# Attention's transposes as pairs of 64 rows, one slot for both products with v, and five edits behind them

## The chip, the core and the metric

The kernel runs on one core of a Trainium2 chip. Its engines work side by side: TensorE (PE in the rows; its weight loads are PEld), VectorE (DVE), ScalarE (ACT), GpSimd (POOL), and SyncE (SP), which issues most of the DMAs. Each engine takes its instructions in program order and waits on semaphores for what the others produce. The metric is the time of one execution on the device in microseconds (us); lower is better.

## The reference

Attention over 32 heads, a first layer, and a second layer in which each token goes to one of 8 experts:

```python
scores = np.matmul(q, k.transpose(0, 1, 3, 2)) / np.sqrt(64)   # q, k, v: 4 x 8 x 576 x 64
decay = cum[..., :, None] - cum[..., None, :]    # cum: running sum of log f
attn = softmax(where(causal, -1e9, scores + decay))
x = (attn @ v).transpose(0, 2, 1, 3).reshape(2304, 512)
h = x @ w_in                                     # 512 x 2048
x = np.maximum(0.01 * h, h) @ w_out              # 2048 x 512
# tokens take experts greedily, in the order of all logits x @ w_gate (2304 x 8);
# an expert takes at most 288 tokens
out[mask] = np.maximum(x[mask] @ w1[e], 0) @ w2[e]   # for each expert e; 512 -> 1024 -> 512
```

## The kernel before

**Precision.** Most operands are kept as a high and a low part in a shortened float32, and a product is three matmuls (high·high, low·high, high·low). Who needs an operand therefore makes two copies of it: `high` rounds (ACT or DVE), `low` subtracts the high part from the source (DVE or POOL).

**Attention (0 to 201.7 us)** treats 16 pairs of heads. For each pair TensorE transposes q and k (128 tokens by the 64 columns of both heads, tile `x`, into PSUM tile `s`); ACT makes the high and DVE the low parts (`qh`, `kh`, `ql`, `kl`); the scores are computed twice, once with the queries in the rows to get the row maximum and the sum of exponentials (DVE's `kept<-s,mask`, ACT's `kept`), and once transposed to give `P = exp(...)`. The log of the sums, computed by a series on POOL (tile `ln`, 10 columns), is transposed by one matmul and goes back as a row of the scores' operand (function `rows`). The products with v (`s<-P,vt`) are left in `xt` by `finish` for the two halves of the queries. All of these share four PSUM slots called `s`.

TensorE can work on parts of its array. The scores use 64 rows by 128 columns (form "S": two heads side by side, shown as 64\*128 and counted as x2), the products with v 128 rows by 64 columns (form "V"), and everything else, the transposes too, the whole array (form "A").

**Order.** Attention and the first layer are laid out by a planner, class `Plan`: every operation is given an engine, a duration in ns, a rank and the slots that it takes, a simulation with list scheduling decides the order, and the program keeps that order on each engine (class `InOrder`, whose line L72 is therefore the line of nearly all instructions in the rows). The planner charges `TURN` (200 ns) for a change of TensorE's form, and prefers an operation of the present form when its rank is at most `near` behind. The ranks come from 12 per pair plus constants (`ZP`, `ZO`, `ZA`, `ZH`, ...). In the changed kernel L72 is L73.

**First layer (201.7 to 690.3 us).** Its weights are read, split into parts that sum exactly (`wsq`, `wbits`, `wst` on POOL and DVE), transposed (`T<-ident,wst`), and multiplied by the gate's parts (`T<-wt,wgs`), so that the logits come out of the same numbers as the reference's. At 442.7 us the logits, laid out as `L`, are brought into the token list `W0`. Then the greedy routing runs on DVE, POOL and ACT (generator `routing`, which yields the ns that it wants covered), while TensorE is dealt the second product of the first layer (`acc<-wh,gh`, `acc<-wh,gl`) between the routing's steps. At its end the lists of tokens (`ids`) come out of products `q_misc<-r_ge`, and POOL gathers the tokens `xe` by indirect DMA. Behind them the experts' weights are already split: `wst` (SP's DMA, four buffers), `wh` high (ACT, L359), `wh` low (POOL, L360).

**Experts (690.3 to 915.5 us).** `first` computes the hidden layer of 128 units, `after` the products with w2, `leave` transposes an expert's 288 rows in three groups of 96 and scatters them to `out`. They are ordered by the tile framework's scheduler.

Of the kernel before, what the change touches and what calls it, by code (L numbers as in the profile page):

```python
# [27 lines left out]
ACB = 4  # L28
# [10 lines left out]
ZP, ZO, ZA, ZH, ZL, ZW, DW = -39, -27, 5, -9.5, -10.5, 63, 14.5  # L39
ZS = 5, 5.5, 7, 0.5, 2.5, 11, 11.5  # L40
ZQ = 1
ZT = 0, 7
ZR = 5.5
MW = 1.5, 0.6
LN = -8.262958294867817e-08, 87.99986188054224, 1.833333338331171, -2.9997760462926015, 1.4995521528324076, -0.33310946991454005
FIN = ("act", "vec"), ("vec", "gp")
# [5 lines left out]
ZN = 0.5, 0, -4, 0, 0, 0, -0.5, 0, 0, 0, 0, 0, 0, 0, 2, 0.5  # L52
ZM = -2.5, -0.5, 0, -1, 0, 0, 0, 0, 0, 0, 0, 1, -1.5, 0.5, 4, -4
ZB = 0, -4, -5, 0, 0, 0.5, -0.5, 0, 0, -3, 0, -4, 0.5, 0, 0, -1
# [37 lines left out]
class Plan:  # L92
# [5 lines left out]
    MOVE = 650, 2600  # L98
# [6 lines left out]
    def op(self, eng, ns, fn, needs=(), rank=0.0, takes=(), uses=(), move=0, plain=False, form="A"):  # L105
        o = Op(eng, ns, fn, [x for x in needs if x is not None], rank)
        o.move, o.form = move, form
# [12 lines left out]
        self.ops.append(o)  # L120
        return o
# [4 lines left out]
    def order(self):  # L126
# [100 lines left out]
def tile_kernel(ctx, tc, q, k, v, f, w_in, w_out, w_gate, w1, w2, out):  # L227
# [34 lines left out]

    def weight_ops(op, pieces, z, st, low_on, keep=None, hold=()):
# [7 lines left out]
        def chunk(c, src):  # L271
# [33 lines left out]
            s = op("gp", 800, square, [o], z, ["wsq"], [wb])  # L305
            sq = s.got[0]
            o = op("vec", 202, b0, [o], z, ["wbits"], [wb])
            bb = o.got[0]
            o = op("vec", 335, b1, [o], z, (), [bb, wb])
            o = op("vec", 335, b2, [o], z, (), [bb, wb])  # L310
            s = op("gp", 816, big, [s], z, (), [sq])
            takes = [] if "b" in st else ["wst"]
            o = op("gp", 687, mul, [s, o] + st.get("o", []), z, takes, [sq, bb] + ([st["b"]] if "b" in st else []))
# [199 lines left out]
    with ExitStack() as c1:  # L513
# [64 lines left out]
        VT = [stp.tile([128, 5, 2, D], FT, name=f"vt{i}") for i in range(2)]  # L578
        pads = []
        for n in range(NS):  # L580
# [16 lines left out]
            if n < 2:  # L597
                op("gp", 150, lambda n=n: gp.memset(VT[n][64:, 4], 0.0), (), 12 * n - 90)
# [3 lines left out]
        def prepare(n, own, z):  # L602
# [9 lines left out]
            def load(j, i):  # L612
# [4 lines left out]
                at_q[j].dma_start(x3[j][:, :, i], src[b, h + i, :512].rearrange("(t p) d -> p t d", p=128))  # L617
# [15 lines left out]
            def part(end, z):  # L633
                mine = {}

                def flip():
                    mine[0] = p = bank()
                    if end:
                        pe.transpose(p[:, 0, :128], x3["end"].rearrange("p s d -> p (s d)"), ident)
                        return  # L640
                    for j in range(2):
                        for t in range(4):
                            pe.transpose(p[:, j, 128 * t:128 * t + 128], x3[j][:, t].rearrange("p s d -> p (s d)"), ident)

                def high(j, c0, w, a):
                    hi = (qh[:, 64:] if j else kh)[:, c0:c0 + w]
                    x = mine[0][:, 0, a:a + w] if end else mine[0][:, j]
# [5 lines left out]
                def low(j, c0, w, a):  # L653
                    hi, lo = ((y[:, 64:] if j else y)[:, c0:c0 + w] for y in ((qh, ql) if j else (kh, kl)))
                    x = mine[0][:, 0, a:a + w] if end else mine[0][:, j]
                    vec.scalar_tensor_tensor(lo, x, 0.125 if j else 1.0, hi, op0=OP.mult, op1=OP.subtract)
                if end:
                    o = op("pe", 109, flip, loads["end"], z, ["s"], buf["end"] + list(sets.values()))
# [4 lines left out]
                for j, c0, w, a in ([(0, 512, 64, 0), (1, 512, 64, 64)] if end else [(0, 0, 512, 0), (1, 0, 512, 0)]):  # L663
                    a_ = op("act", 51 + .833 * w, lambda x=(j, c0, w, a): high(*x), [o], z + ZH, (), [tb, sets[j]])
                    outs[j] += [a_, op("vec", 69 + 1.042 * w, lambda x=(j, c0, w, a): low(*x), [a_], z + ZL, (), [tb, sets[j]])]
# [10 lines left out]
        def rows(x, dst, need, z, uses, duse):  # L676
# [3 lines left out]
            def flip():  # L680
                mine[0] = bank()[:10, 0, :128]
                pe.transpose(mine[0], x(), ident)

            def high():
                mine[1] = at.tile([10, 2, 128], FR, name="xr", tag="xr", bufs=2)
                act.copy(mine[1][:, 0], mine[0])

            def low():
                vec.tensor_tensor(mine[1][:, 1], mine[0], mine[1][:, 0], op=OP.subtract)
            o = op("pe", 107, flip, need, z + 1, ["s"], uses)  # L690
# [6 lines left out]
        def offsets(n, own, z):  # L697
# [70 lines left out]
            def ratio():  # L768
                own["ln"] = x = at.tile([128, 4, 10], FT, name="ln", tag="ln", bufs=2)
                act.activation(x[:, 0], own["sm"].bitcast(I32), AF.Copy, scale=LN[0], bias=LN[1])  # L770
                act.activation(x[:, 1], x[:, 0], AF.Exp)

            def ready():
                x = own["ln"]
                gp.tensor_scalar(x[:, 3], own["sm"], 1e-9, None, op0=OP.add)

            def series():
                x, t = own["ln"][:, 2], own["ln"][:, 1]
                gp.tensor_tensor(t, own["ln"][:, 3], t, op=OP.mult)
# [5 lines left out]
                gp.tensor_tensor(x, x, own["ln"][:, 0], op=OP.add)  # L785
# [3 lines left out]
            p = op("gp", 250, ready, tots + [o], z + ZR, (), [sb, lb])  # L789
            o = op("gp", 2200, series, [o, p], z + ZR, (), [nb, sb, lb])  # L790
            own["max"] = rows(lambda: own["ln"][:, 2], lambda l: qr[32 + l:97 + l:64], [o], z + ZR, [lb], kq)

        def attend(n, own, z):
# [18 lines left out]
            def score(name, blocks, z):  # L812
# [24 lines left out]
                for n, (i, f0, f1) in enumerate(blocks):  # L837
                    sel = []
                    if f0 == 128 * i:
                        w = min(128, f1 - f0)  # L840
                        sel = [op("gp", 137 + 1.75 * w, lambda a=col[n], w=w: causal(a, w), acts, z + 4, (), [pb])]
# [5 lines left out]
            def values(half, i, z):  # L847
                need, pb, name, a, e, x, y = W[half, i]

                def product():  # L850
                    if i == 0:
                        own["av", half] = bank()[:, 0]
                    for u in range(2):
                        pe.matmul(own["av", half][64 * u:64 * u + 64, x:y], own["v"][:, i, u], own["P", name][:, u, a:e],
                                  start=i == 0, stop=i == (2, 4)[half])
                o = op("pe", 4 * (e - a) / 2.4 + 12, product, need + vl + R.get(("av", half), []), z, ["s"] if i == 0 else [],
                       [vb, pb] + R.get(("avb", half), []), form="V")
                if i == 0:
                    R["avb", half] = [o.got[0]]
                R["av", half] = [o]  # L860

            def finish(half, z):
# [22 lines left out]
                if rest == "gp":  # L885
                    o = op("gp", 96 + 3.55 * w, lambda: low(1), [o], z + 1, (), [xb])
                    o = op("gp", 148 + 2.1 * w, lambda: low(0), [o], z + 1, (), [xb])
# [38 lines left out]
    with ExitStack() as c1:  # L926
        gtp = c1.enter_context(tc.tile_pool(name="gt1", bufs=1, reuse_waits="tile"))
        raw[:] = gtp, W64[1]
        psp = c1.enter_context(tc.tile_pool(name="ps1b", bufs=1, reuse_waits="tile", space=PSUM))
# [77 lines left out]
    with ExitStack() as c2:  # L1007
# [14 lines left out]
        with tc.tile_pool(name="ps2", bufs=1, reuse_waits="tile", space=PSUM) as psp, \  # L1022
# [21 lines left out]
            lp = psa.tile([128, 512], FT, name="acc", tag="acc", bufs=ACB)  # L1044

            def tokens(g):
                for i in (2 * g, 2 * g + 1):
                    pe.matmul(lp[:, E * i:E * i + E], L[:, 128 * i:128 * i + 128], sel, start=True, stop=True)
            o = [op("pe", 430, lambda g=g: tokens(g), lasts[g:g + 1], 200) for g in range(NG)]
# [373 lines left out]
```

## Time and profile before

| | us |
|---|---|
| median of 3 runs (lowest, highest) | 925.02 (924.19, 928.3) |
| the profiled execution, its own time | 927.42 |
| its span from the first to the last instruction | 925.7 |
| TensorE busy | 889.4 (96%) |
| VectorE, ScalarE, GpSimd busy | 584.0, 416.6, 457.6 |
| first layer's first product, 201.7 to 442.7: TensorE busy | 237.0 of 241.0 |
| experts, 690.3 to 915.5: TensorE busy | 222.5 of 225.2 |

The profiled execution took 2.4 us more than the median, and 1.7 us of it lie outside the span. Busy shares are averages over stages with different limits. TensorE's granted clock was 0.989 of full speed over the span: full nearly everywhere, and half in a few short stretches.

### The profile page before, as it was taken

Reading aid. Unit: us, or ns where it says so; the run is one execution under the profiler, and the core shown is the slowest. Engines: PE = TensorE matmul, PEld = TensorE weight load, DVE = VectorE, ACT = ScalarE, POOL = GpSimd, SP = SyncE. Lnnn points to the kernel's source line nnn. Section 1 sums busy time; section 2 is a strip of 40 time slices with the busy share of each in tenths; the row PEclk is TensorE's granted clock in tenths of the full one; section 3 lists DMA queues with packets and bytes.
Section 4 is the critical chain, followed back from the end, with each engine's and each line's share of the span. In section 5 each row is a group of like instructions: output and inputs, shape, how many; then the busy total and the mean of one; then the engine's idle time right before and its main releaser. Section 6 shows DMA issues by size and latency. Waiting matters only on the chain.

```text
span 925.7 us, 19093 instructions
## 1 busy us (share of the span) xinstructions
PE 889.4 (96%) x6934; PEld 755.8 (82%) x6934; DVE 584.0 (63%) x1439; ACT 416.6 (45%) x983; POOL 457.6 (49%) x683
## 2 busy tenths in 40 slices
PE   6899999998999999999999999999899999999996
PEld 6688878876877787777777777777689999999996
DVE  8778876517798389323576677766755665556631
ACT  7899999842222233223122222222344555455521
POOL 8588895548997078000645655555662122121101
PEclk9899999999999999999899999999999999999999
DMA  6566654559984384321312212211246765656611
GB/s 128 149 163 172 182 138 120 178 148 339 323 281 148 137 261 134 114 82 46 124 48 70 69 46 69 69 58 58 80 163 190 225 189 177 196 186 194 189 38 35
DMA packets 139967, 132.36 MB, mean 143 GB/s; under 512 B 68480, under 2 KB 106688, under 8 KB 139872
## 3 DMA queue, kind: packets, MB, share of 16 engines
q1 hardware_dynamic: 135600, 121.40, 42.5%
q0 software_dynamic: 3072, 9.44, 3.5%
q8 instruction: 55, 0.90, 0.4%
q10 hardware_dynamic: 1200, 0.30, 0.1%
q14 instruction: 40, 0.33, 0.1%
HBM read 99.84 MB, written 31.08 MB: 141 GB/s over the span
## 4 chain that ended last, share of the span: by engine, by line
PE 69%; issue 11%; POOL 10%; DVE 4%; ACT 2%; DMA 2%; SPq 0%; POOLq 0%; DVEq 0%; ACTq 0%
PE acc L1059 21%; PE h L72 19%; PE s L72 9%; PE h L1141 6%; PE y L1154 6%; POOL wsq L72 3%; PE T L72 3%; PE q_ct L1059 2%; POOL wst L72 2%; POOL ln L72 1%; ACT kept L72 1%; DVE r_ge L1301 1%; DVE kept L72 1%; POOL P L72 1%; POOL out L1162 1%
## 5 line engine op out<-in xcount | busy, mean ns | idle before, releaser
L72 PE MATMUL h<-X,wh 128*128 128x512 f32 (+1 forms) x960 | 209.6, 375 | 0.6 <-DVE xt L72 0.6
L72 PEld LDWEIGHTS h<-X,wh 128*128 128x128 f32 x960 | 165.0, 188 | 37.8 <-DVE g L72 2.7
L1059 PE MATMUL acc<-wh,gh 128*128 128x512 f32 x576 | 188.2, 404 | 0.0
L453 POOL TENSOR_TENSOR gl<-g,gh 128x512 fp32r<-128x512 f32 x64 | 104.9, 1643 | 82.7 <-ACT gh L452 73.9
L1059 PEld LDWEIGHTS acc<-wh,gh 128*128 128x128 f32 x576 | 108.1, 192 | 19.3
L359 ACT CAST wh<-wst 128x512 fp32r<-128x512 f32 x132 | 80.4, 621 | 84.6 <-DMA wst<-in_moe_w 49.4
L1059 PE MATMUL acc<-wh,gl 128*128 128x512 f32 x288 | 117.4, 408 | 0.9 <-POOL gl L453 0.9
L1141 PE MATMUL h<-XE,wh 128*128 128x288 f32 x768 | 116.7, 301 | 0.9 <-DVE XE L1003 0.9
L72 DVE TENSOR_TENSOR wh<-wst,wh 128x512 fp32r<-128x512 f32 x132 | 91.2, 713 | 40.3 <-ACT wh L359 28.1
L452 ACT CAST gh<-g 128x512 fp32r<-128x512 f32 x72 | 44.5, 621 | 155.0 <-PE acc L1059 132.5
L72 ACT ACTIVATE g<-h 128x512 f32<-128x512 f32 (+1 forms) x80 | 44.4, 555 | 154.4 <-PE h L72 154.4
L1141 PEld LDWEIGHTS h<-XE,wh 128*128 128x128 f32 x768 | 105.3, 189 | 1.2 <-DVE XE L1003 1.2
L1154 PE MATMUL y<-eh,wh 128*128 128x288 f32 x512 | 98.3, 296 | 0.0
L72 DVE TENSOR_TENSOR g<-g,h 128x512 f32<-128x512 f32 (+1 forms) x80 | 50.2, 629 | 68.6 <-ACT g L72 68.2
L72 ACT ACTIVATE kept<-kept,nm 128x192 f32<-128x192 f32 (+4 forms) x160 | 88.0, 553 | 2.9 <-DVE nm L72 2.9
L1162 POOL DMA_INDIRECT out<-yo,ids x24 | 24.8, 1034 | 127.0 <-DVE yo L1161 117.9
L1154 PEld LDWEIGHTS y<-eh,wh 128*128 128x128 f32 x512 | 79.7, 188 | 0.0
L72 DVE SCALAR_TENSOR_TENSOR wbits<-w,wbits 128x256 int32<-128x256 int32 x128 | 76.2, 597 | 3.0
L72 DVE CUSTOM_DVE_ANT_0 kept<-s,mask 128x192 f32<-128x192 f32 (+4 forms) x160 | 59.2, 426 | 23.0 <-PE s L72 22.5
L1154 PE MATMUL y<-el,wh 128*128 128x288 f32 x256 | 68.2, 296 | 0.0
L72 POOL TENSOR_TENSOR wst<-wsq,wbits 128x256 f32<-128x256 f32 x64 | 49.6, 775 | 36.4 <-DVE wbits L72 31.5
L1059 PEld LDWEIGHTS acc<-wh,gl 128*128 128x128 f32 x288 | 55.3, 192 | 10.9 <-POOL gl L453 1.3
(228 smaller groups left out, 1594.9 us busy)
## 6 DMA issues: line engine op xcount, KB each, us to landing
wst<-in_moe_w SPq DMA_DIRECT2D x128, 256.0 KB
X<-xd SPq DMA_DIRECT2D x12, 1024.0 KB
g<-gd SPq DMA_DIRECT2D x36, 256.0 KB
w<-in_moe_w_in SPq DMA_DIRECT2D x32, 256.0 KB
w<-in_moe_w_out SPq DMA_DIRECT2D x32, 256.0 KB
gd<-g SPq DMA_DIRECT2D x16, 512.0 KB
xd<-xt SPq DMA_DIRECT2D x16, 320.0 KB
x2d<-xo SPq DMA_DIRECT2D x20, 256.0 KB
```

What stands on the lines that cost most here:

```text
L72: r = getattr(self.engine, name)(*a, **k)
L359: A.copy(r[u][0], x)
L452: A.copy(gh, g)
L453: on.tensor_tensor(gl, g, gh, op=OP.subtract)
L1059: tc.keep_in_program_order(PE.matmul(*a, **k))
L1141: PE.matmul(h[:, :CAP], w, X[:, c, x, :], start=n == 0, stop=n == 3 * NC - 1)
L1154: PE.matmul(yt[c][:, :CAP], w[:, s], a, start=j == 0 and n == 0, stop=j == NJ - 1 and n == 2)
L1162: sd = G.indirect_dma_start(out=out[:, :], out_offset=bass.IndirectOffsetOnAxis(ap=ids[:, 3 * e + t:3 * e + t + 1], axis=0), in_=y, in_off ...
L1301: V.scalar_tensor_tensor(many[:, :NT * (K + 1)].rearrange("p (i k) -> p i k", k=K + 1)[:, :, :K], key[:, :, None].to_broadcast(s), base if ...
```

## The change

1. **Transposes in form S.** Each 128x128 transpose of q, k (and of the `ln` tile) becomes a pair of transposes of 64 rows each, on the upper and the lower half of the array. So that the columns come out in order, q and k are loaded with four consecutive tokens in a partition, and the transposes write PSUM with a step of 8 elements; the high and low copies read it in runs of 4 with a step of 8. k's high copy waits for q's, and both low copies for both high ones. The `ln` tile is one of two fixed tiles of 160 columns that POOL clears once.
2. **One slot `s` for both halves** of a pair's products with v.
3. The copy of the first half of `xt` goes from ACT to DVE (`FIN`). The planner's ranks and a few of its durations are new, and so is the order.
4. **Token list:** 18 products of `L` with a selection matrix and a copy become 18 transposes and 5 sums on DVE.
5. **Routing's end:** the multiplication r_ge<-r_ga,r_ip goes from POOL to ACT, and the first step of the last products asks for 1,400 ns more of cover.
6. **Experts:** `first` does all products with the high part of X before those with the low one.
7. **Last expert:** its last `after` is kept in program order, and its output is transposed column block by column block, left in copies of 384 and 128 columns.

```diff
-ZP, ZO, ZA, ZH, ZL, ZW, DW = -39, -27, 5, -9.5, -10.5, 63, 14.5
+ZP, ZO, ZA, ZH, ZL, ZW, DW = -43.5, -24.5, 7, -3.5, -8.5, 61.5, 23.5
...
-FIN = ("act", "vec"), ("vec", "gp")
+FIN = ("vec", "vec"), ("vec", "gp")
...
-                    same = [x for x in q if x[2].form == form and x[0] <= q[0][0] + self.near]
+                    same = [x for x in q if x[2].form == form and x[0] <= q[0][0] + self.near * x[2].pull]
...
-                at_q[j].dma_start(x3[j][:, :, i], src[b, h + i, :512].rearrange("(t p) d -> p t d", p=128))
+                at_q[j].dma_start(x3[j][:, :, i], src[b, h + i, :512].rearrange("(p t) d -> p t d", t=4))
...
-                            pe.transpose(p[:, j, 128 * t:128 * t + 128], x3[j][:, t].rearrange("p s d -> p (s d)"), ident)
+                        for r in range(2):
+                            d = slice(64 * r, 64 * r + 64)
...
+                                pe.transpose(p[:, r, 4 * j + t::8], x3[j][d, t].rearrange("p s d -> p (s d)"), ident[d, d])
+
+                def turned(j):
...
+                    return mine[0].rearrange("p r (c n) -> p (r c) n", n=8)[:, :, 4 * j:4 * j + 4]
...
-                    o = op("pe", 872, flip, loads[0] + loads[1], z, ["s", "k", "q"], buf[0] + buf[1])
+                    o = op("pe", 888, flip, loads[0] + loads[1], z, ["s", "k", "q"], buf[0] + buf[1], form="S", pull=False)
...
-                pe.transpose(mine[0], x(), ident)
+                p = bank()
+                for r in range(2):
+                    d = slice(64 * r, 64 * r + 64)
+                    pe.transpose(p[:, r, :64], x()[d], ident[d, d])
...
+                    if i == 0 and half == 0:
+                        own["avs"] = bank()
                     if i == 0:
-                        own["av", half] = bank()[:, 0]
+                        own["av", half] = own["avs"][:, half]
...
-                    pe.matmul(lp[:, E * i:E * i + E], L[:, 128 * i:128 * i + 128], sel, start=True, stop=True)
...
+                    pe.transpose(lp[0][:, 128 * (i % 4):128 * (i % 4) + 128], L[:, 128 * i:128 * i + 128], ident)
+
+            def summed(i, lp):
+                n = min(4, NT - i)
+                vec.tensor_reduce(W0[:, :, i:i + n], lp[0][:, :128 * n].rearrange("p (i u e) -> p e i u", u=4, e=32)[:, :E], axis=AX.X, op=OP.add)
...
-                for w, x in ((wh, 0), (wh, 1), (wl, 0)):
...
+            for x in range(2):
+                for c in range(NC):
+                    for w in wa[j // 4][c][:2 - x]:
...
+        for t in range(3):
+            V.tensor_copy(yo[t][:, 384:], p[3][:M, 128 * t:128 * t + 128])
+            send(E - 1, yo[t], t)
...
-    G.tensor_scalar(oa[:, :, 1], ga, ip[:, 0:1], None, op0=OP.mult)
+    nc.scalar.mul(oa[:, :, 1], ga, ip[:, 0:1])
...
-        yield 600
+        yield 600 + 1400 * (i0 == 0)
```

How TensorE's order moves in attention: the end of one round (the last scores of a pair, then transposes, then products with v), before:

```order
L72 MATMUL s<-kr_127,qo 128x288 x2
L72 MATMUL s<-ident,ln 10x128
L72 MATMUL s<-ident,x_114 128x128 x4
L72 MATMUL s<-ident,x_115 128x128 x4
L72 MATMUL s<-P,vt_136 64x320 x2
L72 MATMUL s<-P,vt_136 64x192 x2
L72 MATMUL s<-P,vt_136 64x64 x2
L72 MATMUL s<-P,vt_136 64x256 x6
L72 MATMUL s<-P,vt_136 64x192 x2
L72 MATMUL s<-P,vt_136 64x64 x2
L72 MATMUL s<-ident,x_1141 128x128
L72 MATMUL s<-X 128x320 x8
```

The same place in the change, first the scores' side and then the products with v behind it:

```order
L73 MATMUL s<-ident,x_114 128x64 x8
L73 MATMUL s<-ident,x_115 128x64 x8
L73 MATMUL s<-kh_125,qh_122 128x288 x2
L73 MATMUL s<-kh_125,ql_123 128x288 x2
L73 MATMUL s<-kl_126,qh_122 128x288 x2
L73 MATMUL s<-kr_127,qo 128x288 x2
L73 MATMUL s<-kh_125,qh_122 128x288 x2
L73 MATMUL s<-kh_125,ql_123 128x288 x2
L73 MATMUL s<-kl_126,qh_122 128x288 x2
L73 MATMUL s<-kr_127,qo 128x288 x2
```

```order
L73 MATMUL s<-P,vt_136 64x320 x2
L73 MATMUL s<-P,vt_136 64x192 x2
L73 MATMUL s<-P,vt_136 64x64 x2
L73 MATMUL s<-P,vt_136 64x256 x6
L73 MATMUL s<-P,vt_136 64x192 x2
L73 MATMUL s<-P,vt_136 64x64 x2
L73 MATMUL s<-ident,x_1105 128x64 x2
L73 MATMUL s<-ident,ln_138 128x64 x2
L73 MATMUL s<-X 128x320 x8
```

`x_114` and `x_115` are k and q of a coming pair, `x_1141` and `x_1105` its last 64 tokens, `ln` the logs of the sums, `vt_136` a pair's v, and `X` a set of score operands like `kh` and `qh` in a tile that the first layer uses later. Their transposes and those of `ln` stood between scores and products, or between products and scores, in form A; now they stand in form S at the edge of the scores, and one change of form each way is left in a round. Over attention TensorE changes its form 76 times before and 33 times after.

TensorE in the first layer, at about 222 to 228 us, before and after:

```order
L72 MATMUL T<-ident,wst 128x128 x4
L72 MATMUL h<-X,wh 128x512 x12
L72 MATMUL T<-ident,wst 128x128 x4
L72 MATMUL T<-wt,wgs 32x128 x8
L72 MATMUL h<-X,wh 128x512 x12
L72 MATMUL T<-sel,wq 128x8 x2
L72 MATMUL h<-X,wh 128x512 x12
```

```order
L73 MATMUL T<-ident,wst 128x128 x4
L73 MATMUL h<-X,wh 128x512 x12
L73 MATMUL T<-wt,wgs 32x128 x8
L73 MATMUL T<-ident,wst 128x128 x4
L73 MATMUL h<-X,wh 128x512 x12
L73 MATMUL T<-sel,wq 128x8 x2
L73 MATMUL h<-X,wh 128x512 x12
```

The gate's products `T<-wt,wgs` now stand ahead of the transposes `T<-ident,wst` of the next weights, which stood right before them.

POOL from the end of the routing to the experts, before and after:

```order
L1378 IOTA r_mw 128x18
L360 TENSOR_TENSOR wh<-wst,wh 128x512 x3
L1385 TENSOR_SCALAR r_ge<-r_ga,r_ip 128x18x24
L360 TENSOR_TENSOR wh<-wst,wh 128x512 x3
L997 DMA xe<-x2d,ids 96x512 x3
L360 TENSOR_TENSOR wh<-wst,wh 128x512 x6
L997 DMA xe<-x2d,ids 96x512 x9
```

```order
L1425 IOTA r_mw 128x18
L363 TENSOR_TENSOR wh<-wst,wh 128x512 x8
L1024 DMA xe<-x2d,ids 96x512 x3
L363 TENSOR_TENSOR wh<-wst,wh 128x512 x4
L1024 DMA xe<-x2d,ids 96x512 x9
L1201 DMA out<-yo,ids 2304x512 x3
```

The multiplication `r_ge` has left POOL, and eight subtractions of the weights stand ahead of the first gathers `xe`, where six and the multiplication stood.

## Rows read from the trace of the kernel before

**Rows 1.** Windows: start:end, length, busy PE, PEld, DVE, ACT, POOL; clock; DMA share; GB/s.
```profile
53.03:177.38 124.35, 121.67 (x1512) 107.22 (x1511) 91.12 (x368) 117.97 (x352) 97.32 (x221) 1.00 0.56 147
446.76:690.34 243.58, 237.75 (x1632) 183.39 (x1631) 165.88 (x365) 61.25 (x104) 137.98 (x110) 0.98 0.23 76
```

**Rows 2.** TensorE's timeline in attention: start, length, line, out<-in, tile, shape, count.
```profile
62.68 0.29 PE L72 MATMUL s<-kl,qh 64*128 64x288 f32 x2
62.82 0.29 PE L72 MATMUL s<-kr,qo 64*128 64x288 f32 x2
...
63.29 1.20 PE L72 MATMUL s<-ident,x 128*128 128x128 f32 x9
64.55 0.49 PE L72 MATMUL s<-P,vt 128*64 128x320 f32 x2
```

**Rows 3.** The same timeline cut off at 63.9 us.
```profile
63.29 0.87 PE L72 MATMUL s<-ident,x 128*128 128x128 f32 x6
```

**Rows 4.** TensorE's timeline where scores stand right before products with v.
```profile
183.58 0.28 PE L72 MATMUL s<-ql,kh 64*128 64x64 f32 x2
183.69 0.28 PE L72 MATMUL s<-qr,kr 64*128 64x64 f32 x2
183.90 0.49 PE L72 MATMUL s<-P,vt 128*64 128x320 f32 x2
```

**Rows 5.** ACT's groups in 53.03 to 177.38: busy us, mean ns, idle before.
```profile
L72 ACT ACTIVATE qh<-s 128x512 fp32r<-128x512 f32 x9 | 5.2, 582 | 0.0
...
L72 ACT CAST xt<-s 128x320 fp32r<-128x320 f32 x11 | 4.4, 401 | 0.8 <-PE s L72 0.8
```

**Rows 6.** A group of DVE in the same stretch.
```profile
L72 DVE COPY xt<-s 128x256 f32<-128x256 f32 x11 | 4.6, 414 | 0.1
```

**Rows 7.** DVE's timeline: the copy out of PSUM that reads with a step.
```profile
446.94 0.31 DVE L72 COPY W<-acc 128x144 f32<-128x144 f32 x1 [1.81 <-PE acc L72]
```

**Rows 8.** TensorE's timeline in the first layer; in brackets the wait before.
```profile
226.10 0.44 PE L72 MATMUL T<-ident,wst 128*128 128x128 f32 x2 [1.25 <-POOL wst L72]
...
343.30 0.44 PE L72 MATMUL T<-ident,wst 128*128 128x128 f32 x2 [0.87 <-POOL wst L72]
```

**Rows 9.** Timelines of TensorE and POOL at the token list.
```profile
442.72 4.19 PE L72 MATMUL acc<-sel,L 128*128 128x8 f32 x36
447.05 3.95 POOL L453 TENSOR_TENSOR gl<-g,gh 128x512 fp32r<-128x512 f32 x3 [1.67 <-issue]
```

**Rows 10.** Windows (columns as in group 1): the two stretches at half clock after 440 us.
```profile
447.40:454.20 6.80, 5.90 (x15) 4.63 (x15) 6.77 (x12) 0.62 (x1) 4.43 (x4) 0.50 0.62 195
669.20:672.60 3.40, 3.40 (x20) 2.65 (x19) 1.20 (x1) 0.00 (x0) 3.40 (x3) 0.51 0.30 113
```

**Rows 11.** Timelines of PE, POOL, SP and ACT at the routing's end.
```profile
669.15 0.57 PE L1059 MATMUL q_misc<-r_ge 128*96 128x48 bf16 x6 [2.87 <-POOL r_ge L1385]
...
679.47 0.58 PE L1059 MATMUL q_ct<-ident,xe 96*128 96x96 f32 x4
...
667.29 1.80 POOL L1385 TENSOR_SCALAR r_ge<-r_ga,r_ip 128x432 bf16<-128x432 bf16 x1
669.07 4.24 POOL L360 TENSOR_TENSOR wh<-wst,wh 128x512 fp32r<-128x512 f32 x3
673.68 1.19 POOL L997 DMA_INDIRECT xe<-x2d,ids  x1 [0.37 <-DVE ids L72]
...
670.36 4.21 SPq L354 DMA_DIRECT2D wst<-in_moe_w  x4
...
673.01 0.62 ACT L359 CAST wh<-wst 128x512 fp32r<-128x512 f32 x1 [5.49 <-PE q_misc L1059]
```

**Rows 12.** The tile xe at its first gather: from issue to landing.
```profile
DMA to landing us min/median/max: 4.2/4.2/4.2
```

**Rows 13.** Timelines of PE and POOL: the experts' first gathers, and the last scatter's start.
```profile
697.57 0.36 PE L1132 MATMUL T<-ident,xe 96*128 96x96 f32 x2 [1.76 <-DMA xe<-x2d,ids]
...
917.55 0.92 POOL L1162 DMA_INDIRECT out<-yo,ids  x1 [14.47 <-DVE yo L1161]
```

More of the change, by code (lines that the diff above doesn't have):

```diff
@@ L103, in __init__, with op @@
         self.near, self.linger = near, linger
-    def op(self, eng, ns, fn, needs=(), rank=0.0, takes=(), uses=(), move=0, plain=False, form="A"):
+    def op(self, eng, ns, fn, needs=(), rank=0.0, takes=(), uses=(), move=0, plain=False, form="A", pull=True):
         o = Op(eng, ns, fn, [x for x in needs if x is not None], rank)
-        o.move, o.form = move, form
+        o.move, o.form, o.pull = move, form, pull
         for t in takes:
@@ L261, in tile_kernel @@
     tiny = float(np.array([897 << 20], np.int32).view(np.float32)[0])
+    conv = list(CONV[0])
     def weight_ops(op, pieces, z, st, low_on, keep=None, hold=()):
@@ L578, in tile_kernel @@
         VT = [stp.tile([128, 5, 2, D], FT, name=f"vt{i}") for i in range(2)]
+        lnt = [stp.tile([128, 160], FT, name=f"ln{i}") for i in range(2)]
+        LNS = [{0: x[:, 0:10], 1: x[:, 10:20], 3: x[:, 20:30], 2: x[:, 32:42], 4: x[:, 32:160]} for x in lnt]
         pads = []
@@ L855, in product @@
                                   start=i == 0, stop=i == (2, 4)[half])
[L856 to L859, printed above, removed]
+                o = op("pe", 4 * (e - a) / 2.4 + 12, product, need + vl + R.get(("av", half), R.get("begun", [])), z, ["s"] if i == half == 0 else [],
+                       [vb, pb] + R.get(("avb", 0), []), form="V")
+                if i == half == 0:
+                    R["avb", 0] = R["avb", 1] = [o.got[0]]
+                    R["begun"] = [o]
                 R["av", half] = [o]
@@ L1147, in first, with after @@
             return gh, gl
-        def after(yt, wb, j, gh, gl):
+        def after(yt, wb, j, gh, gl, last):
             wh, wl = wb[j]
@@ L1153, in after @@
                 for n, (w, a) in enumerate(((wh, gh), (wl, gh), (wh, gl))):
-                    PE.matmul(yt[c][:, :CAP], w[:, s], a, start=j == 0 and n == 0, stop=j == NJ - 1 and n == 2)
+                    o = PE.matmul(yt[c][:, :CAP], w[:, s], a, start=j == 0 and n == 0, stop=j == NJ - 1 and n == 2)
+                    if last and j == NJ - 1:
+                        tc.keep_in_program_order(o)
         def leave(e, ys, t):
@@ L1186, in tile_kernel @@
                         g[n, i] = first(X[n], W[n][0], i)
-                after(yt, wb, j, *g[e, j])
+                after(yt, wb, j, *g[e, j], e == E - 1)
                 if ys and j < 3:
@@ L1194, in tile_kernel @@
                 (A.copy if c % 2 else V.tensor_copy)(ys[:, c], yt[c][:, :CAP])
+        p = [ps.tile([128, 512], FT, name=n, tag=n, bufs=2) for n in ("T3", "T3", "h3", "h3")]
+        for c in range(NC):
+            for t in range(3):
+                PE.transpose(p[3][:M, 128 * t:128 * t + 128] if c == NC - 1 else p[t][:M, 128 * c:128 * c + 128], ys[:, c, M * t:M * t + M], ident)
+        yo = [ep.tile([M, DM], FT, name="yo", tag="yo", bufs=3) for _ in range(3)]
         for t in range(3):
-            leave(E - 1, ys, t)
+            (A.copy if t % 2 else V.tensor_copy)(yo[t][:, :384], p[t][:M, :384])
+        for t in range(3):
+            V.tensor_copy(yo[t][:, 384:], p[3][:M, 128 * t:128 * t + 128])
+            send(E - 1, yo[t], t)
 def routing(nc, wk, ids, ps, W0, mm, vec, where):
```

117 lines of the change are left out of this document (66 added, 51 removed).

## The prediction, on record before the change was run

> **What bounds the kernel now.** I read the windows of the stages first [rows 1]. In 53.03 to 177.38 us lie 11 rounds of attention, one for a pair of heads: 124.35/11 = 11.30 us each, in which TensorE is busy 121.67/11 = 11.06, ACT 117.97/11 = 10.72, POOL 8.85 and DVE 8.28. TensorE is the bound with ACT 0.34 us behind it, so an edit pays there by shortening TensorE's queue, and what TensorE gains beyond 0.34 a round pays only if ACT gets shorter too. From 446.76 to 690.34 TensorE is busy 237.75 of 243.58: at most 5.83 us are left to waiting. Second, TensorE's timeline around its changes of form, since a busy TensorE is not one at its peak [rows 2 to 4]. Third, the waits that remain behind attention: for POOL's `wst` in the first layer [rows 8], at the token list [rows 9], and at the routing's end [rows 11]. In the last two of these places the granted clock is half (1.2 GHz) [rows 10].
>
> **Attention, −4.3 us.** From the last pair of scores to the first product with v pass 64.55 − 62.82 = 1.73 us [rows 2]. In it lie that pair's own 0.14 (62.82 − 62.68) and ten transposes, one of `ln` and nine of q and k. Nine take 1.20 us and six 0.87 [rows 2, 3], so one takes 0.33/3 = 0.11, and ten take 1.10. The rest, 1.73 − 0.14 − 1.10 = 0.49, is what the changes of form cost. Where scores stand right before products with v, the last pair takes 183.90 − 183.69 = 0.21 where the pair before it took 0.11 [rows 4]: a change costs 0.10. The new order keeps one such change and drops the others: 0.49 − 0.10 = 0.39 a round. The transposes cost the same as before, ten pairs (four each of q and k, one for the end, one for `ln`) by the 0.11 of a pair of 64x64 scores in place of ten by 0.11. Over 11 rounds that is −4.3 us. The rounds ahead of and behind this stretch wait for loads and weights as well; I count nothing there.
>
> ACT must follow: the copy of the first half of `xt` leaves it, 4.4/11 = 0.40 a round [rows 5]. ACT's 10.72 becomes 10.32, under TensorE's 11.06 − 0.39 = 10.67 by the same margin as now. DVE takes that copy at about its 256-column copy's 0.41 by 320/256 = 0.52 [rows 6] and stands at 8.8; POOL is untouched but for two clearings at the start. One slot in place of two for the products with v gives the scores more room, and that the low copies wait for both high ones delays them by one copy, 0.58 [rows 5], for a pair that is needed rounds later. I take both as nothing. Where DVE's new copy comes late, the shared slot is freed late, and scores wait.
>
> The new high and low copies read PSUM in short runs with a step. No row has an ACT instruction like it; the nearest is DVE's copy that reads with a step, 0.31 us for 144 columns [rows 7], where the 256-column copy's 0.414 [rows 6] would give 0.23 in proportion. It is thus at most 0.31/0.23 = 1.33 times as slow, and some of that is a fixed cost. For two high copies of 0.58 the upper bound is 0.33 × 1.16 = 0.38 a round: ACT 10.70, about level with TensorE. I take no cost, because DVE's row holds a fixed part. The transposes write with a step too. Here 64 columns of a pair stand against 288 columns that take 0.14 [rows 2], while 64 take 0.11 [rows 4]: the columns are hidden under what a pair costs anyway, and even a write four times slower (as if 256 columns) would stay at about 0.14, 0.03 × 9 = 0.3 a round. The Trainium skill, page "PSUM — Partial Sum Buffer", section "Specifications (TRN2)", speaks against this part: PSUM's lines have 8 bytes, and any access that isn't contiguous slows matmuls significantly. No run here shows a strided write of TensorE; rival E works it out. Bounds of this part: 0 to −8 (twice as much, if the rounds at the start and end gain as well).
>
> **First layer, −1.5.** The gate's products now stand ahead of the transposes that wait 1.25 at 226.10, and 12 products `h` ahead of those that wait 0.87 at 343.30 [rows 8]. Twelve products cover the second wait whole; of the first I let the eight short ones cover half: −0.63 − 0.87. Both waits end with POOL, whose chain isn't shorter, so a part can show up later: 0 to −2.1.
>
> **Token list, −2.0.** The 18 products (36 records) fill 442.72 to 446.76 [rows 9, 1], 4.04 us; 18 transposes at 0.11 take 2.0. POOL's `gl`, for which TensorE stands next, comes right after them at 447.05: its tile lies where `L` was, so it moves along. The five sums on DVE are beside it. Bounds −1.6 (by 0.13 each, 1.20/9) to −2.1.
>
> **Half clock behind it, −1.5.** In 447.40 to 454.20 TensorE is busy 5.90 of 6.80 at a clock of 0.50 [rows 10]; at full clock that work is 2.95, so 2.95 are at stake. What stands ahead of it is 4.04 us of products with 8 columns, then a wait of 0.90. With dense transposes and a shorter gap the clock may stay up; half of it is my value, the range 0 to −2.95. The Trainium skill, page "TensorE: Matmul & The Clock Gate", section "Part 4: PE-mode transpose", says that transposes don't count as busy for the clock in the same way; by that the stretch stays, and the sum would be 1.5 less of a gain.
>
> **Routing's end, +0.8.** TensorE waits 2.87 for POOL's multiplication `r_ge`, and the stretch behind is at half clock (3.40 us, 1.7 to be had) [rows 11, 10]. On ACT, idle there for 5.49, the multiplication is done early, and TensorE gains up to 2.87 + 1.7 = 4.6. But next stand the transposes of the gathered `xe` at 679.47, and POOL now does eight subtractions before the gathers. They are chained through four buffers: subtraction 4, which follows at once when the multiplication is gone, ends at 667.29 + 4.24/3 = 668.7; only then SP loads buffer 4 again, which took 673.01 − 670.36 = 2.65 until ACT's copy; this copy of 0.62 and subtraction 7 follow, then 8: 668.7 + 2.65 + 0.62 + 2 × 1.41 = 674.8. The gather, before at 673.68, starts then, and lands 4.2 later [rows 12], a little after 679. Its own path had 679.47 − 673.68 = 5.8 with other work behind it, so TensorE comes at about 679.47 − 4.6 = 674.9 and waits some 4 us for what it had without waiting, and may fall to half clock afterwards (1.7 as above). Gain 4.6, new wait 4.1 to 4.5, and 0 to 1.7 of slow clock: −0.5 to +1.6, taken as +0.8. If DVE or the scheduler leaves the gather where it was, the part is −4.2.
>
> **Experts 0, last expert +0.2.** The order in `first` could start up to 0.5 earlier, but 1.76 us of waiting for the gather of the next `xe` at 697.57 [rows 13] follows and takes it. At the end the rows leave in two copies each, and the third has to wait for the others on DVE: the first scatter, now 917.55 [rows 13], comes 0.2 later (−0.3 to +0.5).
>
> **Sum.** −4.3 − 1.5 − 2.0 − 1.5 + 0.8 + 0.2 = −8.3 against the profiled execution's 927.4, so 919.1 there. It was 2.4 above the median of 925.0; the forecast for the median is 925.0 − 8.3 = **916.7**, for this case alone 913 to 920.
>
> **Rivals.** *A: the gather isn't late or the clock holds.* POOL's chain has slack if a load returns sooner, and TensorE's half-clock stretch after the list goes altogether. Instead of +0.8 the routing's end brings −2.5, instead of −1.5 the clock −2.5: 916.7 − 3.3 − 1.0 = 912. For it speaks ACT's long idle time there; against it the four-buffer chain. *B: attention gives nothing.* TensorE's 0.39 a round turns into waits, for a shared slot that is freed only when DVE has copied both halves, or for ACT, which is 0.35 behind. The 4.3 go: 921.0. For it speaks that all engines are at 73 to 98% there and the order is wholly new; against it, ACT's 0.40. *C: more in attention*, the rounds at the start and the end gain too, and q's and k's loads in pieces four times as long come sooner: −8 there, 913, with A's parts 909. *D, the other side: the strided reads bind ACT.* Its two high copies (1.16 a round) lengthen. The gain elsewhere is 4.0, so the kernel is slower when a round takes over 11.30 + 4.0/11 = 11.66 on ACT, from 10.32: when the copies take (1.16 + 1.34)/1.16 = 2.2 times as long. At three times a round is 12.64, +1.34 × 11 = 14.7 in place of −4.3: 925.0 + 14.7 − 4.0 = 936. DVE's at most 1.33 speaks against it [rows 7]. *E: the strided writes slow the transposes.* Nine pairs a round write with a step. At 0.14 instead of 0.11 they cost 0.3 a round: 916.7 + 3.0 = 920. At 0.25 (as if 512 columns, by the 0.14 of 288) they cost 1.26, TensorE's round is 10.67 + 1.26 = 11.93 with its waits left out, 0.87 over the present 11.06: 925.0 − 4.0 + 9.6 = 931. No row of this kernel has a write like it; against it stands the slack that a pair of 64 columns has.
>
> **Chances.** The forecast's case 0.43, A 0.18, C 0.09, B 0.16, E 0.08, D 0.06. In 0.2 of the forecast's 0.43 the half-clock stretch after the list stays as it is, 916.7 + 1.5 = 918.2. About 0.5%, 4.6 us, is what a measurement can tell from no change: faster is under 920.4, slower over 929.6. Faster: the first three, a third of B, a quarter of E, 0.77. Same: most of the rest, 0.16. Slower: D and the worst of E, 0.07. The range 907 to 923 leaves out D, half of E and the ends of B and C.
>
> **What would show it.** In the new profile, rounds of 10.9 us in attention with TensorE's scores and transposes in one run, ACT at 10.3 a round, high copies of 512 columns at 0.58, pairs of transposes 0.11 apart; the list at 2.0 us; no wait for `r_ge`, but one of some 4 us for `xe`. Wrong would make it: high copies over 0.8, a wait for a slot `s` in each round, or the gather on time.

## The result, and the profile after

The change made the kernel slower: 939.4 us (939.13 to 939.81) against 926.66, ratio 1.0118 (95% interval 1.0085 to 1.0152). The forecast was 916.7, the range 907 to 923, counted from a median of 925.02: −8.3 was forecast and +12.7 measured. The profiled execution's span is 938.1 us, 12.4 more than before, and the stages, each read off TensorE's timeline from its first instruction to that of the next stage, say where:

| us | before | after | forecast | measured |
|---|---|---|---|---|
| attention | 201.70 | 215.45 | −4.3 | +13.75 |
| first layer, first products | 241.02 | 239.25 | −1.5 | −1.8 |
| token list | 4.04 | 1.94 | −2.0 | −2.1 |
| from the list to the experts | 244.53 | 247.56 | −0.7 | +3.0 |
| experts, to the last product | 223.95 | 222.71 | 0 | −1.2 |
| tail | 10.46 | 11.19 | +0.2 | +0.7 |

First the windows of these stages after the change, and of a stretch behind the routing, which answer to [rows 1, 10]; columns as there:

```profile
0.00:215.45 215.45, 182.35 (x2368) 153.30 (x2368) 146.94 (x572) 173.59 (x507) 149.75 (x363) 1.00 0.52 141
53.03:177.38 124.35, 114.70 (x1552) 97.58 (x1549) 96.61 (x380) 114.07 (x342) 98.83 (x222) 1.00 0.54 146
454.70:456.64 1.94, 1.94 (x23) 1.94 (x19) 1.47 (x4) 0.00 (x0) 1.94 (x8) 1.00 0.18 63
456.64:704.20 247.56, 237.49 (x1633) 183.33 (x1631) 165.05 (x370) 62.52 (x108) 138.42 (x112) 0.98 0.24 78
689.00:694.00 5.00, 5.00 (x25) 5.00 (x25) 0.00 (x0) 0.00 (x0) 3.13 (x3) 0.50 0.51 133
```

TensorE's work in attention did fall: it is busy 182.35 us there. But it stands still for 33.1. Before, the same window reads

```profile
0.00:201.70 201.70, 186.43 (x2209) 161.44 (x2209) 140.03 (x557) 177.10 (x523) 147.43 (x361) 0.98 0.57 151
```

which leaves 15.3. The list of TensorE's waits after the change (total us, times, longest) names the new one at the top:

```profile
PE s L73 <- DVE xt L73: 12.7, 19, 0.8
PE s L73 <- POOL ln L73: 6.9, 3, 5.9
PE q_ct L1093 <- DMA xe<-x2d,ids: 5.7, 1, 5.7
PE s L73 <- DVE X L73: 3.6, 1, 3.6
```

Before, TensorE has no wait for `xt` in attention; the list there begins with the wait at the start:

```profile
PE s L72 <- POOL vt L72: 5.8, 1, 5.8
PE s L72 <- DVE nm L72: 2.1, 5, 1.1
```

TensorE's timeline of one round, where [rows 2] stood:

```profile
65.25 0.28 PE L73 MATMUL s<-qr,kr 64*128 64x64 f32 x2
65.36 0.71 PE L73 MATMUL s<-ident,x 64*128 64x64 f32 x16
65.88 0.38 PE L73 MATMUL s<-kh,qh 64*128 64x288 f32 x2
...
66.89 0.29 PE L73 MATMUL s<-kr,qo 64*128 64x288 f32 x2
67.11 2.50 PE L73 MATMUL s<-P,vt 128*64 128x320 f32 x24
70.29 0.66 PE L73 MATMUL s<-P,vt 128*64 128x192 f32 x8 [0.69 <-DVE xt L73]
```

and DVE's timeline beside it:

```profile
69.04 0.68 DVE L73 SCALAR_TENSOR_TENSOR ql<-s,qh 128x512 fp32r<-128x512 f32 x1
69.66 0.49 DVE L73 CAST xt<-s 128x320 fp32r<-128x320 f32 x1
70.06 0.28 DVE L73 TENSOR_SCALAR wbits<-w 128x256 int32<-128x256 int32 x1
70.99 0.49 DVE L73 TENSOR_TENSOR xt<-s,xt 128x320 fp32r<-128x320 f32 x1 [0.64 <-PE s L73]
```

Of the 32 records of a round's products with v, 24 run. The last eight, all of them products of the second half, start right after DVE's copy of the first half (69.66 to 70.15). Then DVE's second read of the first half waits until those eight have run. The halves share no byte, and neither result enters the other.

The priced parts of the transposes hold. Eight pairs take 65.88 − 65.36 = 0.52 us, 0.065 each, less than 0.11, although they write with a step. The copies that read with a step are as long as before [rows 5]:

```profile
L73 ACT ACTIVATE qh<-s 128x512 fp32r<-128x512 f32 x9 | 5.2, 583 | 0.0
L73 ACT CAST kh<-s 128x512 fp32r<-128x512 f32 x9 | 5.2, 575 | 0.0
```

So rivals D and E are out. The routing's end after the change (timelines of TensorE, POOL, DVE, SP and ACT in turn), against [rows 11]:

```profile
688.77 0.53 PE L1093 MATMUL q_ct<-ident,xe 96*128 96x96 f32 x1 [5.66 <-DMA xe<-x2d,ids]
...
669.27 10.62 POOL L363 TENSOR_TENSOR wh<-wst,wh 128x512 fp32r<-128x512 f32 x5 [0.70 <-ACT wh L362]
680.35 3.00 POOL L363 TENSOR_TENSOR wh<-wst,wh 128x512 fp32r<-128x512 f32 x2 [0.46 <-ACT wh L362]
683.53 1.19 POOL L1024 DMA_INDIRECT xe<-x2d,ids  x1 [0.18 <-issue]
...
680.83 1.37 DVE L456 TENSOR_TENSOR gl<-g,gh 128x512 fp32r<-128x512 f32 x1 [3.33 <-ACT gh L455]
682.12 0.17 DVE L1444 COPY r_kf<-q_misc 96x24 f32<-96x24 f32 x1
682.32 0.18 DVE L73 SCALAR_TENSOR_TENSOR ids<-q_misc,r_kf 96x24 int32<-96x24 f32 x1
...
676.91 16.05 SPq L357 DMA_DIRECT2D wst<-in_moe_w  x10
...
679.65 0.62 ACT L362 CAST wh<-wst 128x512 fp32r<-128x512 f32 x1 [4.28 <-DMA wst<-in_moe_w]
```

The wait for `r_ge` is gone, and the gathered `xe` comes 5.66 us late, with the half clock (1.2 GHz) behind it.

### The profile page after: what moved, and what is told of

The parts are those of the page before. It is cut to its first block, busy times and chain, and to the rows that moved or that the text cites. A ratio compares the mean times of both kernels' runs of the same rounds, so it can differ in the third digit from the quotient of the medians.

```text
span 938.1 us, 19292 instructions
## 1 busy us (share of the span) xinstructions
PE 880.4 (94%) x7076; PEld 743.8 (79%) x7076; DVE 591.6 (63%) x1462; ACT 412.9 (44%) x968; POOL 458.3 (49%) x684
## 4 chain that ended last, share of the span: by engine, by line
PE 77%; DVE 9%; POOL 5%; issue 3%; DMA 3%; ACT 2%; SPq 1%; POOLq 0%; DVEq 0%; ACTq 0%
PE acc L1093 19%; PE h L73 17%; PE s L73 12%; PE y L1188 11%; PE h L1175 11%; PE T L73 3%; PE q_ct L1093 2%; DVE wbits L73 2%; DVE r_ge L1348 1%; DVE kept L73 1%; DVE xt L73 1%; POOL wsq L73 1%; ACT kept L73 1%; DMA xe<-x2d,ids 1%; PE T L1195 1%
## 5 line engine op out<-in xcount | busy, mean ns | idle before, releaser
L73 PE MATMUL s<-P,vt 128*64 128x256 f32 (+3 forms) x512 | 53.2, 342 | 15.9 <-DVE xt L73 12.7
```

What stands on the lines that cost most here:

```text
L73: r = getattr(self.engine, name)(*a, **k)
```

## The experiments

All are timed against the kernel before, in three groups: 1 to 4, 5 to 8 and 9 to 12, where its median is 926.63, 927.66 and 927.14 us. Each ratio is within its group. Attention's length is read from each profile in the same way.

**1. The same order, the halves independent.** Nothing moves on any engine; the framework is told that an access to one half and one to the other are independent:

```diff
+            def apart(other, kind, half, o):
+                for x in own.get(("mm" if kind == "rd" else "rd", other), ()):
+                    tc.declare_no_dep(o.ins, x.ins, reason="other bank")
+                own.setdefault((kind, half), []).append(o)
```

> The changed kernel in the same order on every engine, but the accesses to the two halves of the shared slot (which lie in different PSUM banks) are declared independent, so that products with v of one half no longer wait for the copies of the other, nor these copies for those products. Theory T1 (the shared slot is tracked as one tile, and this costs the time): TensorE's 12.7 us of waits for DVE's xt fall under 2 us, attention ends at 203 to 206 us instead of 215.5, the time is 926 to 931 us. Rival T2 (the new order is bad in itself, the xt waits only take the place of others): other waits appear in each round, attention ends after 211 us, the time stays at 935 to 940 us.

926.12 us, ratio 0.9979 (0.9962 to 0.9996); attention 202.55, 12.9 less. T1 holds: the 13.3 us between 939.4 and 926.1 are all that the change had lost. Of TensorE's waits for `xt` this is left:

```profile
PE s L73 <- DVE xt L73: 1.8, 5, 0.6
```

and a round's products run through:

```profile
66.05 2.94 PE L73 MATMUL s<-P,vt 128*64 128x320 f32 x32
```

**2. Two slots again**, all else as in the change:

```diff
                     if i == 0:
-                        own["av", half] = own["avs"][:, half]
+                        own["av", half] = bank()[:, 0]
```

> The changed kernel with the two halves of the products with v in slots of their own again (13 takes of a slot in a round instead of 12); the planner lays out a new order for it. T1: the waits for xt go, attention ends at 202 to 207 us, the time is 925 to 932 us; where it differs from the kernel with independent halves, it is by what a thirteenth take of a slot costs. T2: attention still ends after 211 us, the time is 935 to 940 us.

936.37 us, 1.0101 (1.0084 to 1.0118); attention 213.40. T1's number for it is missed and the rival's came: without the shared slot the new ranks give an order that is 10.85 us longer than with independent halves. The waits for `xt` don't all go either. In this order they stand ahead of scores:

```profile
PE s L73 <- DVE xt L73: 7.4, 12, 1.5
```

The new ranks need the saved take almost as much as they suffer from the wait that came with it.

**3. The shared slot alone in the kernel before**, and **7. the same with independent halves.** The edits are those of the change's part 2 and of experiment 1.

> The kernel before with nothing but the shared slot for both products with v. T1: TensorE waits for the copies of xt 15 to 20 times, attention grows from 201.7 to 209 to 215 us, the time is 933 to 941 us. T2: attention stays within 2 us of 201.7, the time is 924 to 929 us.

> The kernel before with the shared slot alone, and its halves declared independent. T1: the 951 us of the kernel with the shared slot alone fall back to 924 to 930 us, attention to 200 to 206 us. Rival (the planner's order for the shared slot, with the ranks of before, is what costs): attention stays above 215 us, the time above 938 us.

951.02 us, 1.0254 (1.0237 to 1.0271), attention 229.80; and 927.51, 1.0002 (0.9982 to 1.0022), attention 201.61. The dependence costs 28 us of attention in the old order, more than T1 said. Both copies of the first half are waited for here, ACT's in each of the 16 rounds and DVE's in 14, 18.7 us in all; against experiment 7 TensorE's busy time grows as well, from 186.44 to 195.06 us, at a mean clock of 0.97 for 0.98. TensorE's waits and its timeline in experiment 3:

```profile
PE s L72 <- DVE xt L72: 10.2, 14, 0.8
PE s L72 <- ACT xt L72: 8.5, 16, 0.6
```

```profile
74.46 1.08 PE L72 MATMUL s<-P,vt 128*64 128x256 f32 x8 [0.52 <-ACT xt L72]
76.28 0.66 PE L72 MATMUL s<-P,vt 128*64 128x192 f32 x8 [0.74 <-DVE xt L72]
```

In the old order the shared slot itself is worth nothing.

**4. Independent halves, the routing's end as before**, and **5. the multiplication on ACT without the additional cover:**

```diff
-    nc.scalar.mul(oa[:, :, 1], ga, ip[:, 0:1])
+    G.tensor_scalar(oa[:, :, 1], ga, ip[:, 0:1], None, op0=OP.mult)
...
-        yield 600 + 1400 * (i0 == 0)
+        yield 600
```

(4 has both lines, 5 the second alone.)

> The first of these kernels (independent halves) with the end of the routing as before (the multiplication on POOL, 600 ns of cover). If the late gather and the half clock behind it are what the second stage lost: TensorE's wait of 5.7 us for xe goes, the half-clock stretch behind it goes, the wait of 2.9 us for the multiplication and its half-clock stretch come back, and the time is 3 to 6 us under that of the kernel with independent halves. Rival (the late gather costs nothing, since another wait stands behind it): within 1.5 us of it.

> As the kernel with independent halves, with the multiplication on ACT as in the change, but without the 1,400 ns of additional cover. Theory R1 (the cover places a low copy gl, which waits for a weight's load by way of ACT, ahead of ids on DVE, and so the gather comes late): the wait for xe falls from 4.6 to under 2.5 us, the time is 921 to 924 us. Rival R2 (the subtractions that stand ahead of the gather on POOL once the multiplication has left, now seven, are the cause): the wait for xe stays at 4 to 6 us, the time at 925 to 927 us.

921.36 us, 0.9934 (0.9918 to 0.9951), as expected; and 920.77, 0.9929 (0.9902 to 0.9956), a little under R1's range. The edit of the routing's end costs 926.12 − 921.36 = 4.8 us, and the cover is what costs: without it POOL does seven subtractions ahead of the gather, `ids` stand ahead of `gl` on DVE, and TensorE finds `xe` after 0.72 us at full clock. So R1's number came and R2's did not, but R1's path isn't what ended last. In the changed kernel `ids` are there at 682.32 + 0.18 = 682.50, behind `gl`; POOL's eighth subtraction, which the cover brings as well, ends at 680.35 + 3.00 = 683.35, and the gather starts 0.18 later. POOL and TensorE in 5:

```profile
667.49 1.30 POOL L363 TENSOR_TENSOR wh<-wst,wh 128x512 fp32r<-128x512 f32 x1 [0.36 <-ACT wh L362]
668.98 1.42 POOL L1029 DMA_INDIRECT xe<-x2d,ids  x1 [0.18 <-issue]
...
672.68 0.69 PE L1098 MATMUL q_ct<-ident,xe 96*128 96x96 f32 x4 [0.72 <-DMA xe<-x2d,ids]
```

**6. The first half's copy back on ACT** (`FIN` as before, on top of 4).

> Independent halves and the routing's end as before (921.4 us), with the first half's copy of xt back on ACT. If ACT is close enough to TensorE to bind, as the prediction has it: ACT's round is 10.8 us again, rounds grow by 0.2 to 0.4 us and the time to 923 to 926 us. Rival (ACT has room, and DVE gains it): 919 to 922 us.

921.54 us, 0.9934 (0.9909 to 0.9958), attention 202.37 against 202.04 in 4: no difference. ACT is no bound here.

**8. The pairs alone** (with the order of the high and low copies that part 1 of the change brings): ranks, durations, slots and `FIN` of before.

> Attention with nothing changed but the transposes (pairs of 64 rows in form S): two slots, ranks, durations and the copy of the first half on ACT as before; the token list and the experts are those of the change, the routing's end that of before, and only attention's length is read. The prediction's sum: attention 196 to 199 us (201.7 less 4.3). Rival (what TensorE saves at its changes of form, the planner's order gives back as waits unless the ranks are fitted again): 201 us or more.

946.54 us, 1.0193 (1.0153 to 1.0232), attention 229.91: the rival. Rounds last 8.2 to 19.9 us where they lasted 10.6 to 12.8. In the longest, TensorE stands still for 3.5 of 19.8 us and runs partly at half clock, and no engine is busy throughout:

```profile
55.50:75.30 19.80, 16.27 (x198) 14.02 (x196) 14.62 (x57) 15.10 (x48) 18.00 (x34) 0.91 0.53 144
```

**9. The parts of X independent** (on top of 5). X holds six operands of a pair in one tile, and a DMA writes rows of one of them.

> As the kernel with independent halves and the multiplication on ACT without more cover (920.8 us), and in addition the parts of the tile X (high, low and the rows that a DMA writes) declared independent of each other. If the start is late because a copy into X waits for the DMA into other rows of it: the first scores start at 11 to 13 us instead of 15.1, attention ends 1 to 3 us earlier, the time is 918 to 920 us. Rival (the first scores' start is covered by later waits): attention within 0.7 us of 202.3, the time the same.

920.0 us, 0.9934 (0.9912 to 0.9956). The mechanism shows: the scores `s<-X` follow at 11.07, not 15.08,

```profile
10.97 0.36 PE L73 MATMUL s<-ident,x 64*128 64x64 f32 x1 [1.85 <-DMA x<-in_q]
11.07 0.96 PE L73 MATMUL s<-X 64*128 64x192 f32 x6
```

but of this 0.3 us are left when the second pair's products with v start (53.6 against 53.9), and attention ends at 201.16, 1.1 earlier than in 5. Experiment 11, with the same order in attention, ends at 203.20, so one profile can't show a gain of this size; nor does the time. Mostly the rival.

**10. The token list alone in the kernel before** (the change's part 4).

> The kernel before with the token list alone changed. The prediction: 2.0 us less for the list. If transposes keep the clock up as matmuls do, the half-clock stretch behind the list (6.8 us) goes as well and the time falls by 4.5 to 5.5 us in all, to 921 to 923 us; if they do not count for the clock, the stretch stays and the time falls by 1.5 to 2.5 us.

925.46 us, 0.9978 (0.9954 to 1.0002): 1.7 less than before, the number of the second case, though the interval reaches from nothing to 4.3 less. The profile shows what the first case names: the list takes 1.94 us and the stretch behind it is at full clock,

```profile
445.00:452.00 7.00, 5.69 (x25) 4.32 (x25) 6.93 (x15) 0.68 (x2) 5.92 (x7) 1.00 0.82 261
```

and from the list to the product with `r_ge` it takes 220.07 in place of 222.39, 2.3 less. The profile's span is only 2.4 shorter all the same (923.3), because a stretch at half clock, 693.9 to 697.3, falls into the experts there, which take 225.86 in place of 223.95.

**11. The last expert's output as before, and 12. the selects ahead of the weights' work on POOL** (both on top of 9, 12 on top of 11):

```diff
-                        sel = [op("gp", 200 + 1.68 * w, lambda a=col[n], w=w: causal(a, w), acts, z + 4, (), [pb])]
+                        sel = [op("gp", 200 + 1.68 * w, lambda a=col[n], w=w: causal(a, w), acts, z - 2, (), [pb])]
```

> The kernel with the parts of X independent, and the last expert's output as before the change (three groups of 96 rows, each left in one copy). The tail behind the last product was 10.46 us before and 11.2 in the change: the time falls by 0.7 us against the kernel with the change's tail; rival: the product order of the last expert made up for it, no difference.

> The same with the causal selects on POOL ranked ahead of the weights' work (rank z - 2 instead of z + 4). In every version of the change one round of attention lasts 12.7 to 14.6 us because a select stands behind two subtractions of weights on POOL. If that is what the round lost: no round over 12 us in the middle of attention, and 2 to 4 us less than without it. Rival: POOL's work is only moved, and TensorE waits for wst or ln in its place, no gain.

920.19 us, 0.9920 (0.9894 to 0.9946), and 919.97, 0.9920 (0.9889 to 0.9951). The tail is 10.92 instead of 11.19, too little to be seen in the time. In 12 the round that lasted 14.6 us (14.4 in 11) lasts 12.6, not under 12 as expected, and attention 200.18 instead of 203.20 (201.16 in 9); the time shows nothing of it. Independent halves, the multiplication on ACT and no more cover (experiment 5) make the version that beats both kernels, the one before by some 0.7% and the changed one by some 2%; what I added to it can't be told from noise.

## Why the prediction was wrong

**The step that failed is the sentence that one slot for both products "gives the scores more room" and is taken as nothing.** It priced the slot's room and not what sharing does to the semaphores. The framework orders accesses by tile: a write to one half waits for a read of the other. The planner, which took the halves as independent, put DVE's copy of the first half among the second half's products, so 15 of the 16 rounds wait for about 0.7 us, and the last four twice. Taking this away in the same order gives back 13.3 us (experiment 1); bringing it into the old order costs 23.5 (951.02 against 927.51). The prediction's own sign of being wrong, "a wait for a slot `s` in each round", came nearly as named. Rival B had the place, "a shared slot that is freed only when DVE has copied both halves", but the wrong reason (the slot's release) and therefore the wrong bound: it let the wait eat the 4.3 us of gain and no more. Priced by the row at hand, a copy of some 0.5 us to be waited for in each of 16 rounds, B would have reached 8 us further, 929.

**Attention, −4.3:** TensorE's own share came, its gain did not. Its busy time falls from 186.43 to 179.61 us in experiment 1; attention stays at 202.55. These are the windows of the 11 rounds of [rows 1] in experiment 1, and of one of them:

```profile
54.90:179.30 124.40, 118.90 (x1612) 102.10 (x1612) 96.72 (x387) 116.71 (x352) 100.86 (x233) 0.99 0.55 149
99.20:113.80 14.60, 12.30 (x150) 9.98 (x148) 8.53 (x36) 10.57 (x33) 11.95 (x33) 0.88 0.51 140
```

The 11 rounds take 124.40 us, as long as the 124.35 of before. The one lasts 14.6 where it lasted 10.84 (98.94 to 109.78); the other ten are 3.7 us shorter together, 0.37 each, close to the forecast's 0.39. That the size fits is in part luck: from start to start and without its waits, TensorE spends 0.57 us a round less on transposes and changes of form there, in part because a pair takes 0.065 and not 0.11, and 0.19 more on scores and products with v. What came in ten rounds of eleven is lost at two places that the sum put at nothing. The first scores start at 15.08 instead of 10.37 (experiment 9), of which 1.85 are left at the second pair's products with v (54.87 for 53.02); and the long round waits for a select behind two subtractions of weights on POOL, with half clock after it (12). Behind the eleven rounds 1.1 us are gained. In experiment 12 both places cost less, 1.5 and 1.8, and attention is 200.18, 1.5 under the kernel before. The long round's wait in experiment 1:

```profile
102.30 0.91 PE L73 MATMUL s<-P,vt 128*64 128x192 f32 x10 [2.30 <-POOL P L73]
```

Experiments 2 and 8 show more: the order that the planner finds moves attention by 10 to 28 us with edits that were priced at tenths of a microsecond a round. Why it finds such orders without the fitted ranks stays open.

**ACT must follow:** over attention ACT's busy time falls from 177.10 to 171.57 us (experiment 1), 0.35 in each of 16 rounds, near the forecast's 0.40. It was no bound, though: with the copy back on ACT nothing changes (6).

**First layer and list** came near the forecast (−1.8 for −1.5, −2.1 for −2.0). In the first layer that is in part luck: of the 4.0 us of waits for POOL's `wst` 0.7 are left, more than the two waits priced, but 1.9 us of waits for DVE's `g` are new.

**Half clock behind the list, −1.5:** 2.3 (10). The stretch is at half clock in the profiles of all three kernels with the old list and in none with the transposes. The gap behind the list isn't what decides: TensorE waits 1.31 us for `gl` behind the transposes, more than the 0.90 of before. In experiment 7 the clock falls while the old list's products still run, in a list from 443.34 to 448.16:

```profile
443.34:446.40 3.06, 3.06 (x32) 3.05 (x28) 0.92 (x2) 0.00 (x0) 2.67 (x10) 1.00 0.24 74
446.60:448.10 1.50, 1.50 (x9) 1.50 (x9) 0.00 (x0) 0.00 (x0) 0.00 (x0) 0.50 0.66 231
```

After the 18 transposes in 1.94 us the clock stays at 1.00. By the rule of the Trainium skill, page "TensorE: Matmul & The Clock Gate", section "Part 4: PE-mode transpose", that transposes don't count as busy in the same way, the stretch would have stayed. Whether they do count, or are only over sooner than the 4.04 us of products, no run here tells.

**Routing's end, +0.8:** the mechanism was right and its sum too small; the edit costs 4.8 (4 against 1). POOL's first subtraction there, before and after, gives the time by which everything there is later, 7.87 us:

```profile
659.37 1.33 POOL L360 TENSOR_TENSOR wh<-wst,wh 128x512 fp32r<-128x512 f32 x1 [4.02 <-ACT wh L359]
...
667.24 1.33 POOL L363 TENSOR_TENSOR wh<-wst,wh 128x512 fp32r<-128x512 f32 x1 [4.02 <-ACT wh L362]
```

With it the chain through the reload of a weights' buffer ran nearly as told: the load is issued at 676.91 (668.7 + 7.87 = 676.57 by the forecast), ACT's copy follows 2.74 later (2.65), and the gather starts at 683.53 (674.8 + 7.87 = 682.67). That 2.65 was luck, since the copy in its row had waited for TensorE and not for its load [rows 11]. On the side, `ids` came 4 us after the last products that they need, behind `gl`, `gh` and ACT's copy of that weight. TensorE's wait was 5.66 for 4.1 to 4.5. The term that was mis-sized most is the slow clock behind it, put at 0 to 1.7: TensorE works at half clock from 688.77 to about 696.3, 7.5 us, so some 3.8 are lost. −4.6 + 5.66 + 3.8 is 4.9. The end of that stretch lies in this window, half for 2.3 of its 6 us:

```profile
694.00:700.00 6.00, 6.00 (x23) 4.88 (x23) 0.00 (x0) 0.62 (x1) 0.00 (x0) 0.81 0.17 65
```

**Experts 0, tail +0.2:** −1.2 and +0.7. Where no half-clock stretch falls into it, this stage takes 222.5 to 223.0 us in eight kernels with the new order in `first`, 223.6 in a ninth (8), and 223.9 to 224.6 in the three with the old one. The order is a likely source; it wasn't tried alone. In the tail the first scatter starts 2.59 us after the start of the last product where it was 2.31: 0.3 later, as told. The rest of the 0.7 lies behind it and isn't the edit's alone, for with the same tail experiments 2, 6 and 8 take 10.74 instead of 11.19.

**Chances:** the case on the other side had 0.07, and it was none of the mechanisms named that came.

## What to carry to other kernels

When two results move into one tile, read the waits that the framework puts on their accesses before pricing the room that it saves: tracked by tile, readers of one half and writers of the other wait for each other, and a planner that doesn't know it schedules them into each other. An edit of a kernel laid out by a planner is worth what the whole new order is worth: a saving priced from one round came in ten rounds of eleven and was lost in the eleventh and at the start. When an instruction is moved off a queue, look at what moves up in its place and at what stands behind that on the other engines.

## What the runs showed that I had not expected

Transposes of 64 rows in pairs, written with a step of 8 words, take 0.065 us a pair, against 0.11 for 128x128 ones [rows 2, 3] and for a pair of 64x64 scores [rows 4]. By the Trainium skill, page "PSUM — Partial Sum Buffer", section "Specifications (TRN2)", an access that isn't contiguous slows matmuls significantly; nothing of that shows here, nor in ACT's reads with a step (583 ns for 512 columns, 582 without). A wait of TensorE of 2.3 us was followed by half clock (0.88 over the 14.6 us of its round in experiment 1), and one of 5.66 by half clock up to 696 us, over more than 7 us.
